# Hash matmuls moved beside the row sums, two pairs ahead, in a hash-bucket attention kernel

## The chip, the cores and the metric

The kernel runs on one core of a Trainium2 chip. The metric is the device time of one launch in microseconds, the median of several runs. Each time is that of the core from launch to end; the profile's span, a little shorter, runs from the first to the last instruction.

## The reference

Two blocks follow each other. The first is attention for 4 batches and 8 heads, 768 positions and 64 dimensions a head, in which a query sees only the keys of its own hash bucket:

```python
q_bits = (np.einsum('bhsd,dk->bhsk', q, proj) > 0)      # proj: 64 x 6
k_bits = (np.einsum('bhsd,dk->bhsk', k, proj) > 0)
q_bucket, k_bucket = (np.sum(b * 2 ** np.arange(6), axis=-1) for b in (q_bits, k_bits))
scores = np.where(q_bucket[..., :, None] == k_bucket[..., None, :], q @ k.T / 8, -1e9)
attn = softmax(scores);  attn_out = attn @ v
```

The second is a feed-forward block on the 3072 rows of 512 that come out of it:

```python
h = x @ w_in                                   # 512 -> 2048
g = h * (1.0 / (1.0 + np.exp(-1.702 * h)))
out = g @ w_out                                # 2048 -> 512
```

## The kernel before

Attention works on 16 **pairs** of heads: pair n holds two heads of one batch, head j on partitions 64j to 64j+63. The 768 queries of a pair are cut into two **halves** c of 384, its keys into 6 tiles of 128. The main loop (line 553) runs over pairs 1 to 15; pair 0 is written out ahead of it, interleaved with the start of pair 1's work. After the loop the feed-forward part takes over, which uses a seven-product scheme in two stages (lines 712 and 824) and keeps its own order.

The order of instructions on TensorE, VectorE, ScalarE and GpSimd is that of the program text, since the kernel turns the scheduler off for these four (`tc.manual_schedule(engines=ORDERED)`, line 72). SyncE's queue, which issues nearly all loads, is filled by the framework; its issues run in order too, so a load that waits holds up those behind it.

What one pair needs, by the names of the code:

- `fetch(n, name)` (line 317) loads the pair's keys or queries as rows, into one buffer for each of the two. `fetch_v(n)` (line 330) loads values, into two buffers in turn.
- `turn(n, name)` (line 388): VectorE transposes them in 32 x 32 blocks to columns, kT and qT, which have two buffers each (`wk`, bufs=2). The buffer of pair n+2 is that of pair n.
- `measure(n, name)` (line 393): ScalarE squares and sums the raw rows. It serves a guard at the end (`guard`, line 516), which picks another form of softmax if the inputs are very large.
- `hashed(n)` (line 402): four TensorE matmuls of 128 x 32, one for each quarter of the 128 columns (keys and queries, both halves), with the weights `pf`. They write the PSUM tile `hash`, of the pool `mps` that has one bank.
- `featured(n)` (line 411): VectorE makes 0 or a large number of each dot product (`f`), and eight small DMAs bring `f` to the layout of the score matmuls, kf and qf. These have two buffers, `feats[n % 2]`.
- `scores(n, c, tiles)` (line 423): for each key tile, two bf16 matmuls of the features (they add a large positive number where buckets agree) and two f32 matmuls of keys and queries, each on 64 rows of the array, into the PSUM tile `ps` (two banks; the pool `sps` has three such tiles). ScalarE then takes the exponential into `es[c]` (line 433).
- `add_low` and `add_high` (lines 437 and 443) add the exponentials over the key tiles: GpSimd the first three (lines 440, 441), VectorE the other three and GpSimd's sum (lines 446, 448), into `acc`.
- `values(n, c, tiles)` (line 450): 12 f32 matmuls of 128 x 64 into the PSUM tile `av`, for c = 0 in the one bank of the pool `aps`, for c = 1 in the bank of `mps`, which it shares with the hash. `unload(n, c)` (line 466) is ScalarE's copy of `av` into `xT`.
- `total(n)` (line 472): four matmuls of 128 x 32 with a matrix of ones, which sum `acc` over partitions into `dn`, in the bank of `aps`. Its first two need add_high of c = 0, the others that of c = 1.
- `invert(n)` (line 481) turns `dn`, takes reciprocals and turns them back into `rs`; `norm(n)` (line 497) multiplies `xT` by it, all on VectorE.
- `begin(n)` and `step(n, 6)` (lines 508, 504) convert one chunk of w_in per pair from 64-bit to 32-bit numbers: a load, then six VectorE instructions (lines 178 to 198) and one on ScalarE (line 190) that waits for the second of them.

TensorE in pair n of the loop runs scores of both halves, hash of pair n+1, values of both halves, sums. The few lines that set VectorE's order around them:

```python
inverted = invert(n - 1)
next(inverted)
if 1 < n < last:
    turn(n + 1, "k")
whole(inverted)
...
if n < last:
    turn(n + 1, "q")
add_high(n, 0)
if n < last:
    hashed(n + 1)
    featured(n + 1)
...
    norm(n - 1)
add_high(n, 1)
```

Of the kernel before, what the change touches and what calls it, by code (L numbers as in the profile page):

```python
# [19 lines left out]
P = 128  # L20
# [18 lines left out]
def kernel(  # L39
# [243 lines left out]
    def attention(ff):  # L283
# [4 lines left out]
        with actx:  # L288
# [28 lines left out]
            def fetch(n, name):  # L317

                b, hp = pairs[n]
                x = raws[n, name] = ld.tile([P, S // 32, 32], F32, tag=name, name=name)  # L320
                if (n, name) == (2, "q"):
                    behind(x[:, 0, 0:1])
                src = {"k": k, "q": q}[name]
                for j in range(2):
                    rows = src[b, 2 * hp + j].rearrange("(s p) (a i) -> a p s i", p=32, i=32)
                    for a in range(D // 32):
                        r0 = D * j + 32 * a
                        loader[0].dma_start(out=x[r0 : r0 + 32], in_=rows[a])
# [59 lines left out]
            def turn(n, name):  # L388
                x = raws[n, name]
                xt = xts[n, name] = wk.tile([P, S], F32, tag=f"{name}T", name=f"{name}T")  # L390
                nc.vector.transpose(xt, x.rearrange("p s i -> p (s i)"))

            def measure(n, name):

                x = raws.pop((n, name))
                i = 2 * n + "kq".index(name)
                junk = st.tile([P, S], BF16, tag="junk", name="junk", bufs=1)
                nc.scalar.activation(junk, x.rearrange("p s i -> p (s i)"), Act.Square, accum_out=sizes[:, i : i + 1])
# [3 lines left out]
            def hashed(n):  # L402

                h = dots[n] = mps.tile([P, HS], F32, tag="m", name="hash")
                for i, x in enumerate("kq"):
                    for c in range(2):
                        r0 = D * i + 32 * c
                        nc.tensor.matmul(h[r0 : r0 + 32, :], pf[x], xts[n, x][:, c * HS : (c + 1) * HS],  # L408
                                         start=True, stop=True)

            def featured(n):
                f = wk.tile([P, HS], BF16, tag="f", name="f", bufs=1)
                nc.vector.tensor_scalar(f, dots.pop(n), above[:, 0:1], weight[:, 0:1], op0=Alu.is_gt, op1=Alu.mult)
                for c in range(2):
                    for i, x in enumerate("kq"):

                        queue = nc.scalar if (n, x, c) == (1, "q", 0) else nc.sync
                        for j in range(2):
                            r0 = D * i + 32 * c + 2 * NB * j
                            queue.dma_start(out=feats[n % 2][x][D * j : D * j + 2 * NB, c * HS : (c + 1) * HS],  # L420
                                            in_=f[r0 : r0 + 2 * NB, :])

            def scores(n, c, kts):
                qT, kT, qf, kf = xts[n, "q"], xts[n, "k"], feats[n % 2]["q"], feats[n % 2]["k"]
                cols = slice(c * HS, (c + 1) * HS)
                for kt in kts:
                    ps = sps.tile([P, 2, 512], F32, tag="s", name="ps")
                    keys = slice(kt * P, (kt + 1) * P)
                    for a, m, last in ((kf, qf, False), (kT, qT, True)):
                        for j in range(2):  # L430
                            hs = slice(D * j, D * (j + 1))
                            nc.tensor.matmul(ps[:, j, 0:HS], a[hs, keys], m[hs, cols], start=not last, stop=last)  # L432
                    nc.scalar.activation(es[c][:, kt, :, 0:HS], ps[:, :, 0:HS], Act.Exp, scale=1.0 / D**0.5)  # L433
# [16 lines left out]
            def values(n, c, kts):  # L450
                if 0 in kts:

                    pool, tag = (mps, "m") if c else (aps, "av")
                    avs[n, c] = pool.tile([P, HS + 1], F32, tag=tag, name="av")
                av, vt = avs[n, c], vts[n]
                for t in kts:
                    for j in range(2):
                        nc.tensor.matmul(av[D * j : D * (j + 1), :], vt[:, t, j, :], es[c][:, t, j, :],  # L458
                                         start=(t == 0), stop=(t == T - 1))
# [6 lines left out]
            def unload(n, c):  # L466
                av = avs.pop((n, c))
                vs = st.tile([P, 1], F32, tag="vs", name="vs")
                nc.scalar.copy(vs, av[:, HS : HS + 1])
                nc.scalar.activation(x_of(n)[:, c * GT : (c + 1) * GT, :], av[:, 0:HS].rearrange("p (t s) -> p t s", t=GT), Act.Identity, bias=vs[:, 0:1])  # L470

            def total(n):

                dn = accs[n] = aps.tile([P, HS], F32, tag="av", name="dn")
                for c in range(2):
                    acc = accs.pop((n, c))
                    for j in range(2):
                        r0 = D * j + 32 * c
                        nc.tensor.matmul(dn[r0 : r0 + 32, :], ones[:, 0:32], acc[:, j, :], start=True, stop=True)  # L479

            def invert(n):


                rt = st.tile([P, HS // 32, 32], F32, tag="rt", name="rt", bufs=1)
                nc.vector.transpose(rt.rearrange("p s i -> p (s i)"), accs.pop(n))
                yield
                r = st.tile([P, 2, HS // 32], F32, tag="r", name="r")
                nc.vector.reciprocal(r, rt[:, :, 0].unsqueeze(1).to_broadcast([P, 2, HS // 32]))
                for r0 in range(0, P, 32):
                    c = r0 // 32 % 2  # L490
                    r1 = r0 + 32 - 64 * c
                    nc.vector.reciprocal(r[r1 : r1 + 32, c], rt[r0 : r0 + 32, :, 0])
                rs = accs[n] = st.tile([P, S], F32, tag="rs", name="rs", bufs=1)
                nc.vector.transpose(rs.rearrange("p (s i) -> p s i", i=32),
                                    r.rearrange("p c s -> p (c s)").unsqueeze(2).to_broadcast([P, S // 32, 32]))

            def norm(n):
                x, rs = x_of(n), accs.pop(n)
                nc.vector.tensor_tensor(x, x, rs.rearrange("p (t s) -> p t s", t=T), op=Alu.mult)  # L499
# [4 lines left out]
            def step(n, count=1):  # L504
                for _ in range(count):
                    next(conv.get(n, iter(())), None)
# [40 lines left out]
            fetch(2, "q")  # L547
            fetch_v(1)
            scores(0, 1, high)
            values(0, 1, low)  # L550
            values(0, 1, high)
            unload(0, 1)
            for n in range(1, last + 1):
                scores(n, 0, every)
                add_low(n, 0)
                if n == 1:
                    add_high(0, 1)
                    turn(2, "k")
                    total(0)
                inverted = invert(n - 1)  # L560
                next(inverted)
                if 1 < n < last:
                    turn(n + 1, "k")
                whole(inverted)
                if n == last:
                    guard(0)
                scores(n, 1, every)
                add_low(n, 1)
                if n < last:
                    turn(n + 1, "q")  # L570
                add_high(n, 0)
                if n < last:
                    hashed(n + 1)
                    featured(n + 1)
                    for x in "kq":
                        measure(n + 1, x)
                else:
                    guard(1)
                if n < last:
                    norm(n - 1)  # L580
                add_high(n, 1)
                if n == last:
                    norm(n - 1)
                values(n, 0, every)
                unload(n, 0)
                step(n, 6)
                values(n, 1, every)
                unload(n, 1)
                total(n)
                if n + 2 <= last:  # L590
                    for x in "kq":
                        fetch(n + 2, x)
                if n < last:
                    fetch_v(n + 1)
                    begin(n + 1)
                if n > last - len(x_sums):
                    x_sums[n - last - 1]()
# [378 lines left out]
    def whole(steps):  # L976
        for _ in steps:
            pass
# [46 lines left out]
```

## Time and profile before

| What | Value |
|---|---|
| Time, median of 3 runs | 875.63 us (875.22 to 876.58) |
| Span of the profiled run | 873.4 us |
| Attention, first instruction to the first feed-forward matmul | 321.2 us |
| TensorE busy | 862.0 us |
| VectorE busy | 718.4 us |
| ScalarE busy | 312.1 us |
| GpSimd busy | 321.4 us |
| Granted TensorE clock | 0.996 of full speed |

In the profile PE is TensorE's matmuls, PEld its weight loads, DVE VectorE, ACT ScalarE, POOL GpSimd and SP SyncE. A line of the matmul records gives the start and length in us, the engine, the line of the code, the operation, what it writes and reads, the rows and columns of the array that it uses (128*32 is a tile of all rows and 32 columns), the size and the count. An f32 matmul leaves two records. An entry in square brackets is idle time of the engine just before, and what ended it. The chain of work that ended last is followed back from the last instruction to whatever released each step; in order of time it shows which engine the end of the kernel hung on at each moment.

### The profile page before, as it was taken

The page shows a single profiled execution, that of the slowest core. Times are in us where ns is not written, and L with a number is a line of the kernel's source. Part 1 is how long each engine was busy: PE and PEld are TensorE (multiplying, and loading weights), DVE is VectorE, ACT ScalarE, POOL GpSimd, SP SyncE. Part 2 cuts the span into 40 slices and gives each one's busy share as a digit, 9 for nine tenths or more (in the row PEclk, how much of TensorE's full clock was granted, in tenths as well). Part 3 has the DMA queues.
Part 4 walks back from the last instruction along what each step waited for, and adds up shares of the span by engine and source line. Part 5 has one row for each costly group of instructions (what it writes and reads, how often), then busy time and mean ns, then how long its engine had stood idle before and what let it go on. Part 6 is the DMA issues. An engine that isn't in the chain of part 4 may idle for free.

```text
span 873.4 us, 11818 instructions
## 1 busy us (share of the span) xinstructions
PE 862.0 (99%) x4077; PEld 501.8 (57%) x4077; DVE 718.4 (82%) x1020; ACT 312.1 (36%) x519; POOL 321.4 (37%) x275
## 2 busy tenths in 40 slices
PE   9999999999999999999999999999999999999995
PEld 5444444444444444444444444444888888888884
DVE  4579999998999988778777778888888977897785
ACT  5756577777666653222233222332000000000000
POOL 4243334334433375665543344659903100000000
PEclk9999999999999999999999999999999999999998
DMA  5334456544444304565455555575844675467524
GB/s 133 59 59 84 84 102 101 117 89 83 83 84 91 75 25 158 192 217 193 175 193 185 205 181 202 183 249 184 298 167 155 197 250 197 163 200 241 193 97 99
DMA packets 169155, 131.99 MB, mean 151 GB/s; under 512 B 123616, under 2 KB 138112, under 8 KB 163712
## 3 DMA queue, kind: packets, MB, share of 16 engines
q1 hardware_dynamic: 166528, 129.70, 51.6%
q10 hardware_dynamic: 2560, 1.46, 0.7%
q8 instruction: 34, 0.56, 0.3%
q14 instruction: 33, 0.27, 0.1%
HBM read 79.69 MB, written 50.33 MB: 149 GB/s over the span
## 4 chain that ended last, share of the span: by engine, by line
PE 96%; DVE 3%; issue 0%; ACT 0%; ACTq 0%; DVEq 0%
PE product L712 33%; PE product L824 27%; PE ps L432 18%; PE av L458 14%; PE dn L479 1%; PE hash L408 1%; DVE xT L828 1%; PE tp L366 1%; DVE y L804 1%; DVE acc L448 0%; DVE xT L499 0%; PE warm L359 0%; PE hash L373 0%; DVE acc L446 0%; ACT e L433 0%
## 5 line engine op out<-in xcount | busy, mean ns | idle before, releaser
L433 ACT ACTIVATE e<-ps 128x768 f32<-128x768 f32 x192 | 150.6, 812 | 17.2 <-PE ps L432 14.9
L432 PE MATMUL ps<-qT,kT 64*128 64x384 f32 x768 | 155.1, 483 | 0.0
L712 PE MATMUL product<-xT,w_in_sb 128*128 128x512 f32 x288 | 135.5, 593 | 0.0
L458 PE MATMUL av<-e,v 128*64 128x385 f32 x768 | 128.2, 488 | 0.0
L440 POOL TENSOR_TENSOR acc<-e 128x768 f32<-128x768 f32 x32 | 51.3, 1604 | 192.2 <-ACT e L433 116.9
L720 ACT ACTIVATE c<-c 128x512 f32<-128x512 f32 x72 | 45.3, 630 | 184.9 <-issue 78.6
L458 PEld LDWEIGHTS av<-e,v 128*64 128x64 f32 x768 | 53.9, 136 | 72.8 <-issue 71.9
L712 PEld LDWEIGHTS product<-xT,w_in_sb 128*128 128x128 f32 x288 | 54.7, 190 | 68.9 <-issue 64.2
L712 PE MATMUL product<-t_x,s_in 128*128 128x512 f32 x192 | 90.2, 592 | 0.0
L432 PEld LDWEIGHTS ps<-qT,kT 64*128 64x128 f32 x768 | 68.1, 188 | 38.3 <-issue 37.9
L219 POOL TENSOR_TENSOR v<-c,u 128x512 f32<-128x512 f32 x24 | 34.1, 1422 | 121.1 <-ACT c L720 121.1
L837 ACT COPY u<-product 128x256 f32<-128x256 f32 x21 | 7.8, 372 | 172.1 <-PE product L824 138.9
L441 POOL TENSOR_TENSOR acc<-acc,e 128x768 f32<-128x768 f32 x32 | 64.1, 2002 | 2.5
L432 PE MATMUL ps<-qf,kf 64*128 64x384 bf16 x384 | 62.9, 324 | 0.1
L712 PEld LDWEIGHTS product<-t_x,s_in 128*128 128x128 f32 x192 | 36.5, 190 | 45.9 <-issue 43.7
L446 DVE SCALAR_TENSOR_TENSOR acc<-e 128x768 f32<-128x768 f32 x32 | 50.6, 1582 | 5.1 <-ACT e L433 5.1
L712 PE MATMUL product<-t_x,w_in_sb 128*128 128x512 f32 x96 | 45.1, 592 | 0.0
L712 PE MATMUL product<-xT,s_in 128*128 128x512 f32 x96 | 45.1, 592 | 0.0
L432 PEld LDWEIGHTS <-kf 64*128 64x128 bf16 x384 | 19.2, 94 | 35.1 <-issue 11.7
L448 DVE TENSOR_TENSOR acc<-acc,acc 128x768 f32<-128x768 f32 x32 | 31.2, 974 | 4.8 <-POOL acc L441 1.6
L824 PE MATMUL product<-raw_g,xT 128*128 128x256 f32 x152 | 35.1, 379 | 0.0
L448 DVE TENSOR_TENSOR acc<-acc,e 128x768 f32<-128x768 f32 x32 | 31.8, 995 | 3.8 <-ACT e L433 0.5
(207 smaller groups left out, 1495.1 us busy)
## 6 DMA issues: line engine op xcount, KB each, us to landing
raw_g<-g_dram SPq DMA_DIRECT2D x22, 1024.0 KB
s_in<-g_dram SPq DMA_DIRECT2D x20, 1024.0 KB
g_dram<-c SPq DMA_DIRECT2D x72, 256.0 KB
g_dram<-t SPq DMA_DIRECT2D x48, 256.0 KB
raw<-in_moe_w_in_dram SPq DMA_DIRECT2D x16, 512.0 KB
raw<-in_moe_w_out_dram SPq DMA_DIRECT2D x16, 512.0 KB
v<-in_v_dram SPq DMA_DIRECT2D x32, 192.0 KB
g_dram<-u SPq DMA_DIRECT2D x24, 256.0 KB
```

What stands on the lines that cost most here:

```text
L219: return [lambda: eng.tensor_tensor(t1, b12, b11, op=Alu.subtract), lambda: eng.tensor_tensor(b12, b22, b12, op=Alu.subtract), lambda: eng ...
L366: nc.tensor.matmul(tp[D * j : D * (j + 1), i * P : (i + 1) * P], x[name][:, j, c * GT + i, :], ident, start=True, stop=True)
L432: nc.tensor.matmul(ps[:, j, 0:HS], a[hs, keys], m[hs, cols], start=not last, stop=last)
L433: nc.scalar.activation(es[c][:, kt, :, 0:HS], ps[:, :, 0:HS], Act.Exp, scale=1.0 / D**0.5)
L440: nc.gpsimd.tensor_tensor(acc, es[c][:, 0, :, 0:HS], es[c][:, 1, :, 0:HS], op=Alu.add)
L441: nc.gpsimd.tensor_tensor(acc, acc, es[c][:, 2, :, 0:HS], op=Alu.add)
L446: nc.vector.scalar_tensor_tensor(acc, e[0], T * TINY, e[1], op0=Alu.add, op1=Alu.add)
L448: nc.vector.tensor_tensor(acc, acc, x, op=Alu.add)
L458: nc.tensor.matmul(av[D * j : D * (j + 1), :], vt[:, t, j, :], es[c][:, t, j, :], start=(t == 0), stop=(t == T - 1))
L712: nc.tensor.matmul(ps, wq[LEFT[i]][:, kc, :], xq[RIGHT[i]][:, kc, :], start=(kc == 0), stop=(kc == K2 - 1))
L720: nc.scalar.activation(c, c, Act.Gelu_apprx_sigmoid)
L824: nc.tensor.matmul(ps, wq[LEFT[i]][:, c, :], gq[RIGHT[i]][:, c, :], start=(c == 0), stop=(c == F4 - 1))
```

## The change

The hash of a pair is computed two pairs ahead instead of one, and its matmuls stand directly ahead of the matmuls of the sums, which use the array in the same tiles. So that the turned keys and queries are there two pairs ahead, both turns move to the phase of the second half ("on columns"), after add_high(n,0), and norm(n-1) moves from there into the phase of the first half ("on rows"), after the inversion. The raw keys and queries are then fetched three pairs ahead, and values are fetched ahead of the features on the queue. Since the hash's bank is in use for longer, av of the second half takes one of the three score tiles in pairs 1 to 13. Pair 1 does the work of catching up: hash(2) in the old place, hash(3) in the new one.

```diff
             def measure(n, name):
-                x = raws.pop((n, name))
+                x = raws[n, name]
...
             def values(n, c, kts):
                 if 0 in kts:
-                    pool, tag = (mps, "m") if c else (aps, "av")
-                    avs[n, c] = pool.tile([P, HS + 1], F32, tag=tag, name="av")
+                    if c and n == 0 or c and n + 2 > last:
+                        avs[n, c] = mps.tile([P, HS + 1], F32, tag="m", name="av")
+                    elif c:
+                        avs[n, c] = sps.tile([P, 2, 512], F32, tag="s", name="av1")[:, 0, 0 : HS + 1]
+                    else:
+                        avs[n, c] = aps.tile([P, HS + 1], F32, tag="av", name="av")
...
             scores(0, 1, high)
+            measure(2, "k")
...
                 if n == 1:
                     add_high(0, 1)
-                    turn(2, "k")
+                    for x in "kq":
+                        turn(2, x)
+                    fetch(3, "k")
                     total(0)
-                inverted = invert(n - 1)
-                next(inverted)
-                if 1 < n < last:
-                    turn(n + 1, "k")
-                whole(inverted)
+                    measure(2, "q")
+                    fetch(3, "q")
+                    fetch_v(2)
+                whole(invert(n - 1))
+                norm(n - 1)
                 if n == last:
                     guard(0)
                 scores(n, 1, every)
                 add_low(n, 1)
-                if n < last:
-                    turn(n + 1, "q")
                 add_high(n, 0)
-                if n < last:
-                    hashed(n + 1)
-                    featured(n + 1)
+                if n == 1:
+                    hashed(2)
+                    featured(2)
+                if n + 2 <= last:
                     for x in "kq":
-                        measure(n + 1, x)
-                else:
+                        turn(n + 2, x)
+                        measure(n + 2, x)
+                if n == last:
                     guard(1)
-                if n < last:
-                    norm(n - 1)
                 add_high(n, 1)
-                if n == last:
-                    norm(n - 1)
                 values(n, 0, every)
                 unload(n, 0)
                 step(n, 6)
+                if n + 3 <= last:
+                    for x in "kq":
+                        fetch(n + 3, x)
+                if 1 < n < last:
+                    fetch_v(n + 1)
                 values(n, 1, every)
                 unload(n, 1)
+                if n + 2 <= last:
+                    hashed(n + 2)
                 total(n)
                 if n + 2 <= last:
-                    for x in "kq":
-                        fetch(n + 2, x)
+                    featured(n + 2)
                 if n < last:
-                    fetch_v(n + 1)
                     begin(n + 1)
```

## The prediction

> **What bounds the kernel now.** I read the page first for busy shares and for the chain that ended last, then the chain in order of time, then the matmuls one by one where the chain leaves TensorE or changes what it does.
>
> ```profile
> PE 862.0 (99%) x4077; PEld 501.8 (57%) x4077; DVE 718.4 (82%) x1020; ACT 312.1 (36%) x519; POOL 321.4 (37%) x275
> ...
> PE 96%; DVE 3%; issue 0%; ACT 0%; ACTq 0%; DVEq 0%
> ```
>
> TensorE is busy for 99% of the span and is 96% of the chain; VectorE's 82% is an average over both halves. So the time can fall only where TensorE waits or spends time without streaming, and can rise only where it is made to wait. The chain in order of time, start, length, what:
>
> ```profile
> 50.01 0.97 DVE acc L448
> 50.98 0.04 issue
> 51.02 0.84 PE dn L479 x4
> 51.86 9.80 PE ps L432 x72
> 61.66 0.78 PE hash L408 x8
> 62.44 7.92 PE av L458 x48
> 70.35 0.78 PE dn L479 x8
> 71.13 9.80 PE ps L432 x72
> ```
>
> This is the steady state: from pair 2 on, every pair is 9.80 + 0.78 + 7.92 + 0.78 = 19.28 us of TensorE with nothing between, up to 321.16 us, where the feed-forward part starts. Nothing the diff edits runs later than the first microseconds of that part. The one place behind 12 us where attention leaves TensorE is the end of pair 1, at 39.7 to 51.0 us of the chain, which comes back to TensorE at 51.02.
>
> Inside a block there are small steps. The matmuls where scores end, hashes run and values begin (start, length, engine, line, op, tile, shape, count):
>
> ```profile
> 118.68 0.81 PE L432 MATMUL ps<-qT,kT 64*128 64x384 f32 x4
> 119.42 0.52 PE L408 MATMUL hash<-kT,pf_k 128*32 128x384 f32 x2
> 119.43 0.52 PE L408 MATMUL hash<-qT,pf_q 128*32 128x384 f32 x2
> 119.76 0.49 PE L408 MATMUL hash<-kT,pf_k 128*32 128x384 f32 x2
> 119.78 0.49 PE L408 MATMUL hash<-qT,pf_q 128*32 128x384 f32 x2
> 120.20 0.54 PE L458 MATMUL av<-e,v 128*64 128x385 f32 x2
> ```
>
> Look at starts, not lengths. The hash is two rounds on four column groups; round two starts 0.34 after round one. A third round would start at 120.10, but the values start at 120.20. So 0.10 of the block's 0.78 is the change from 128*32 tiles to 128*64. The same holds for the sums (dn starts at 128.12, the next scores at 128.90: 2 x 0.34 + 0.10), and the score block: 12 tiles at the 0.807 from start to start is 9.68, and 0.12 remains of 9.80. A pair has four such changes. Where scores hand over to values directly, in pair 0, it is no dearer: its blocks of three tiles take 2.53 = 3 x 0.807 + 0.11.
>
> **What the Trainium skill says.** "TensorEngine Tiling (Array Packing)", Key Properties: changing the tiling mode, not merely the tile, drains TensorE. The trace agrees: 0.10 to 0.12 us at each change, and 0.34 from round to round within a mode, where 384 columns are streamed. "Perfetto Trace Analysis", Tensor Engine Instruction: TensorE's end times are estimated. The trace agrees (a 0.52 matmul is followed after 0.34 in the same group), which is why I use starts. "SBUF — State Buffer", Who interferes with whom: VectorE and GpSimd share a port pair under an exclusive lock. The trace agrees: line 446 takes 0.92 us alone, and 2.43 when it starts at 122.36 beside GpSimd's add at 121.70.
>
> **The change part by part.**
>
> *Hash beside the sums.* Before, hash(n+1) lies between scores and values in pairs 1 to 14: scores, hash, values, sums, four mode changes. After, hash(n+2) comes just ahead of the sums: scores, values, hash, sums. Both are 128*32, so one change goes. Pair 1 still has hash(2) in the old place and gets hash(3) in the new one; pairs 2 to 13 have one in the new place; pair 14 has none. The number of hashes stays 14, and 13 of them have moved. A mode change that has no row of its own in this place is bounded: 0 saved if hash and sums still part by 0.10, 0.12 if the dearest change goes. I take 0.10, since round to round within a mode is plain in the trace: 13 x 0.10 = **1.3 us**.
>
> *The end of pair 1.* Here the sums wait:
>
> ```profile
> 49.87 0.84 PE L479 MATMUL dn<-acc,ones 128*32 128x384 f32 x4
> 51.02 0.84 PE L479 MATMUL dn<-acc,ones 128*32 128x384 f32 x4 [0.31 <-DVE acc L448]
> 51.79 0.34 PE L432 MATMUL ps<-qf,kf 64*128 64x384 bf16 x2
> ```
>
> The sums take 51.79 - 49.87 = 1.92 instead of 0.78: 1.14 lost, though only 0.31 is called idle, because the second half of the rows comes after the first and not beside it. It waits for VectorE's add_high(1,1), ready at 50.97. In the new order VectorE does turn(2,q) (0.94) in the 3.63 us in which it now waits for the first sums, then from 36.35: inversion to 39.2 (as now); norm(0), 1.4 with GpSimd idle (its 2.61 includes 1.2 behind GpSimd's add of 43.63 to 45.17), to 40.6; add_high(1,0), 3.0, to 43.6; features 0.7, to 44.3; the two turns of pair 3, 1.9, to 46.2; add_high(1,1), 3.0, plus 0.7 behind GpSimd's second add, to 49.9. TensorE now puts hash(3) first, so it reaches the sums at 49.87 + 0.68 = 50.55, and the result is there 0.6 earlier. I take the whole **1.14**; the bounds are 0 and 1.14. The keys for turn(3) are asked for when turn(2,k) is done (32.7), behind the values of pair 1, which end on the queue at 34.7, and the queries after measure(2,q) (37.4); in the trace a turn could start 2.6 us after the last issue of such a load, so by 42.5, ahead of 44.3.
>
> *Turns and norm swapped on VectorE.* The same instructions as before. A pair costs VectorE 17.5 to 18.2 us:
>
> ```profile
> core 0: us, PE busy (x) PEld busy (x) DVE busy (x) ACT busy (x) POOL busy (x), PEclk, DMA share, GB/s
> ...
> 109.69:128.97 19.28, 19.28 (x138) 9.01 (x140) 17.92 (x24) 13.62 (x23) 7.04 (x4) 1.00 0.55 95
> ```
>
> The new waits: turn(n+2) writes the buffers that scores(n,1) read, so it must wait for their end, 9.8 us into the pair. Behind it stand add_high(n,1), the conversion of w_in and f(n+2). VectorE comes to it at about 10.6: conversion to 2.6, f, inversion, norm and add_high(n,0), 0.7 + 2.8 + 1.4 + 3.1 later. From there 1.9 + 3.0 to 4.5 bring add_high(n,1) to 15.5 to 17, and the sums need it at 18.5. So no wait reaches TensorE: **0**. The waits that go (up to 0.9 for the hash, 0.2 to 0.7 for keys) were VectorE's own and buy nothing either.
>
> *av of the second half in a score buffer.* The third score tile of the next pair now waits until ScalarE has unloaded av, 1.6 us into the pair. Before, that unload ended at 110.69, 1.07 into the pair, held up by line 190, which waits for VectorE's conversion; the new order brings that conversion forward. **0**, with 0.5 us of room even if it does not.
>
> *Loads.* Values and the next keys go ahead of the features on the queue; features are needed a whole pair later than they are issued (16 us ahead, not 8). **0**. The first pair's measure(2,k) and measure(2,q), 1.03 each, move into ScalarE's waits (0.95 before the second half's first exponential, and before the unload at 30.8). **0**.
>
> Sum: 875.63 - 1.3 - 1.14 = **873.2 us**.
>
> **The rivals.**
>
> *Half of it.* If the sums of pair 1 still wait as long: 875.63 - 1.3 = 874.3. If hash and sums still drain between each other but the wait goes: 875.63 - 1.14 = 874.5. For the first: that moment depends on where GpSimd's locks fall, and two turns are added ahead of it. Against: 0.6 us of room. For the second: a wait on TensorE's own semaphore stands between hash and sums in the program; against: what it waits for is av of the first half, done 4 us before.
>
> *VectorE becomes the bound.* Its slack is 19.18 - 17.9 = 1.3 per pair. If the new order makes add_high(n,0) also meet GpSimd's add (0.92 to 2.43, plus 1.5) and leaves 0.4 of gaps, a pair takes 17.9 + 1.9 = 19.8, 0.6 too long for 12 pairs: 873.2 + 7.4 = 880.6, slower. For it: norm moves next to GpSimd's first adds. Against: those end about 6 us into the pair, when norm is just starting, and norm leaves the place where it was blocked.
>
> **Numbers.** Forecast 0.66, half of it 0.22, VectorE bound 0.12. The first gives 872.5 to 873.9, the second up to 874.8; with 0.2 either side, the range 872.3 to 875.0 leaves out the third and little else. 0.2% is 1.75 us, so the bar is 873.88: the forecast clears it by 0.7, both halves miss it. Faster 0.66, same 0.22, slower 0.12.
>
> **What would show it.** Right: pairs of 19.18 on the chain (9.80, 7.92, then 1.46 for hash and sums), sums starting 0.34 after the hash's second round, no TensorE idle about 50 us, the feed-forward part starting near 318.7. Wrong: hash and sums still 1.56 together; sums with an idle time ended by acc L448; scores waiting for the unload of av; VectorE with no idle in a pair and pairs above 19.28.

## The result, and the profile after

| | before | after |
|---|---|---|
| time, median (lowest to highest), us | 875.64 (874.88–876.58, 6 runs) | 871.63 (871.17–871.79, 6 runs) |
| ratio, 95% interval | | 0.9954 [0.9941, 0.9967] |
| span of the profiled execution, us | 873.43 | 869.93 |
| VectorE busy, us | 718.4 | 722.4 |

The kernel is 4.0 us faster; the forecast was 2.4. TensorE is still busy for 99% of the span and is still 96% of the chain that ended last. Cut at three instructions on TensorE and VectorE, the two profiled spans compare like this (head: to the first score matmul; attention: from there to the first feed-forward matmul; feed-forward: to the end of the last transpose into y; tail: to the end of the span):

| us | head | attention | feed-forward | tail |
|---|---|---|---|---|
| before | 10.53 | 310.57 | 544.96 | 7.38 |
| after | 10.81 | 307.64 | 545.00 | 6.48 |
| difference | +0.28 | **−2.93** | +0.04 | **−0.90** |

The 0.28 of the head is within its scatter: the profiles of before and of the six kernels built on it have heads of 9.74 to 11.24 (mean 10.53), and those of after and its five 9.97 to 10.81 (mean 10.42). What is left, 2.93 + 0.90 = 3.83, agrees with the gain of 4.0 within its interval (2.9 to 5.2).

**Attention** on the chain of waits of after, in order of time (start, us, engine, tile, line, count):

```profile
41.52 0.78 PE hash L408 x8
42.31 7.92 PE av L463 x48
50.22 0.78 PE hash L408 x8
51.01 0.65 PE dn L484 x8
51.65 9.80 PE ps L432 x72
61.45 7.92 PE av L463 x48
69.36 0.78 PE hash L408 x8
70.15 0.65 PE dn L484 x8
...
318.52 288.60 PE product L722 x672
```

Pair 1 has two hashes, at 41.52 and 50.22, and goes from its values straight into hash and sums, with no wait on VectorE. From then on a pair is 9.80 + 7.92 + 0.78 + 0.65 = 19.15 on the chain; from the first sums to the next on the timeline it is 19.14, against 19.28 before. Feed-forward starts at 318.52 instead of 321.16 (less the 0.28 of the head, 2.93 earlier). The block of hash and sums on TensorE's timeline (start, length, line, tile, shape, count):

```profile
107.57 0.52 PE L408 MATMUL hash<-kT,pf_k 128*32 128x384 f32 x2
107.59 0.52 PE L408 MATMUL hash<-qT,pf_q 128*32 128x384 f32 x2
107.92 0.49 PE L408 MATMUL hash<-kT,pf_k 128*32 128x384 f32 x2
107.93 0.49 PE L408 MATMUL hash<-qT,pf_q 128*32 128x384 f32 x2
108.24 0.83 PE L484 MATMUL dn<-acc,ones 128*32 128x384 f32 x8
109.00 0.34 PE L432 MATMUL ps<-qf,kf 64*128 64x384 bf16 x2
```

Read the starts: 107.57, 107.92, 108.24, and 109.00 for the next scores. The first round takes 0.35 to the second, but the second takes only 0.32 to the third. That third is the first round of the sums, another tile, another line, and no step between. Hash and sums together are 109.00 − 107.57 = 1.43; before they were 0.783 + 0.785 = 1.568.

**VectorE** waits in all of 51 to 300 us for these (what waits, for what; us in total, times, longest). First the two largest waits of before, then all of after:

```profile
DVE kT L391 <- DMA k<-in_k_dram: 7.3, 10, 3.2
DVE f L413 <- PE hash L408: 4.4, 8, 0.6
```

```profile
DVE f L413 <- DMA qf<-f: 1.9, 1, 1.9
DVE acc L448 <- POOL acc L441: 1.6, 1, 1.6
```

The two waits of before, 11.7 us over some 13 pairs, are gone. VectorE's advance over TensorE is seen in the room between the end of VectorE's last sum and the start of the dn matmuls that read it. In pairs 2 to 13 this room was 0.5 to 1.4 us before (0.54 and 0.60 in pairs 2 and 3) and is 2.15 in almost every pair now. In pair 1 it was −1.09 (TensorE waited) and is 0.26.

**The tail.** The two kernels end on the same operations. The last transpose into y, and the span with its mean clock, first of before and then of after:

```profile
865.42 0.63 DVE L804 STREAM_TRANSPOSE y<-xT 128x256 f32<-128x256 f32 x1
...
core 0: 873.4 us, clock 0.996
```

```profile
862.82 0.63 DVE L814 STREAM_TRANSPOSE y<-xT 128x256 f32<-128x256 f32 x1
...
core 0: 869.9 us, clock 0.997
```

From the end of this transpose to the end of the span it is 7.38 before and 6.48 after. The difference shows at the barrier that closes the program, where the engines wait for each other; it stands in the trace's semaphore records and in no line of the page. In before, SyncE, ScalarE and TensorE pass the barrier at 871.87 and VectorE only at 873.09, 1.22 later; in after all four pass it at 869.35 to 869.36. An instruction fetch lies close to the barrier in both (872.19 and 869.41), so its presence alone does not tell the two apart.

### The profile page after: what moved, and what is told of

It is laid out like the page before. It is cut to its first block, busy times and chain, and to the rows that moved or that the text cites. A ratio compares the mean times of both kernels' runs of the same rounds, so it can differ in the third digit from the quotient of the medians.

```text
span 869.9 us, 11937 instructions
## 1 busy us (share of the span) xinstructions
PE 859.7 (99%) x4077; PEld 502.2 (58%) x4077; DVE 722.4 (83%) x1020; ACT 313.4 (36%) x519; POOL 312.7 (36%) x275
## 3 DMA queue, kind: packets, MB, share of 16 engines
q10 hardware_dynamic: 2560, 1.46, 0.8%
## 4 chain that ended last, share of the span: by engine, by line
PE 96%; DVE 3%; issue 0%; ACTq 0%; ACT 0%; DVEq 0%
PE product L722 33%; PE product L834 26%; PE ps L432 18%; PE av L463 15%; PE hash L408 1%; PE dn L484 1%; DVE y L814 1%; DVE xT L838 1%; PE tp L366 1%; DVE t_x L838 0%; PE warm L359 0%; PE hash L373 0%; DVE t2a L221 0%; DVE raw_g L220 0%; DVE v L838 0%
## 5 line engine op out<-in xcount | busy, mean ns | idle before, releaser
L441 POOL TENSOR_TENSOR acc<-acc,e 128x768 f32<-128x768 f32 x32 | 55.7, 1740 | 2.5
L446 DVE SCALAR_TENSOR_TENSOR acc<-e 128x768 f32<-128x768 f32 x32 | 48.8, 1524 | 5.1 <-ACT e L433 5.1
L448 DVE TENSOR_TENSOR acc<-acc,e 128x768 f32<-128x768 f32 x32 | 34.4, 1075 | 3.3
```

The source lines that it names most:

```text
L441: nc.gpsimd.tensor_tensor(acc, acc, es[c][:, 2, :, 0:HS], op=Alu.add)
L446: nc.vector.scalar_tensor_tensor(acc, e[0], T * TINY, e[1], op0=Alu.add, op1=Alu.add)
L448: nc.vector.tensor_tensor(acc, acc, x, op=Alu.add)
```

## The experiments

The theory formed on these readings has three terms: 1.78 us (13 pairs x 0.137) from changes of the array's mode, that is, of the tile shape in which TensorE works; 1.14 from pair 1's wait, which stays away only because VectorE got room in the later pairs too; and 0.90 from where VectorE's instruction stream happens to end. Rivals: VectorE owes the 1.14 in any case and only the place is new; the tail is scatter or depends on the loads; the hash's distance of two pairs pays by itself. Each kernel is one edit of before or of after; ratios are to before, timed on the same chip.

**1 and 2. The tail.** Into a branch that is never taken, VectorE instructions are added: 68 in before, which is by how many the change makes VectorE's program longer, and 60 in after, which makes 128 together. Nothing that runs is changed.

```diff
     with tc.If(unsafe, preferred_fallthrough_block=False):
+        for _ in range(68):     # 60 in the kernel after
+            nc.vector.memset(ones[0:1, 0:1], 1.0)
         with tc.tile_pool(name="cv3", bufs=1) as cv:
```

> The kernel before, with 68 tiny VectorE memsets in the branch that is never taken: nothing that runs is changed, only where the end of VectorE's instruction stream lies (68 is by how many instructions the change makes it longer). Theory of the tail (VectorE waits about 1.2 us for its last instructions to be fetched): 1.2 us off, 874.4 us, and in the profile VectorE's last semaphore instruction comes as early as the other engines'. Rival (the rest of the gain is scatter in how loads land at the start and stores at the end): no change, 875.6 us.

> The changed kernel, with 60 such memsets in the branch that is never taken, which puts VectorE's end where it was before, modulo 128 instructions. Theory of the tail: 1.2 us back, 872.8 us. Rival (scatter): 871.6 us.

Measured: before with 68 is 874.49, ratio 0.9989 [0.9981, 0.9998], its tail 6.48 where it was 7.38 and its attention 310.58. After with 60 is 872.28, ratio 0.9964 [0.9951, 0.9978], its tail 7.35, its attention 307.64. The times alone show the first of the two; the interval of the second overlaps that of after. The tails show both, before with 68 first and after with 60 second:

```profile
865.37 0.63 DVE L804 STREAM_TRANSPOSE y<-xT 128x256 f32<-128x256 f32 x1
...
core 0: 872.5 us, clock 0.997
```

```profile
861.94 0.63 DVE L814 STREAM_TRANSPOSE y<-xT 128x256 f32<-128x256 f32 x1
...
core 0: 869.9 us, clock 0.997
```

So 0.9 us of this change is no effect of the new order: dead instructions give it to the old kernel and take it from the new one. All 13 profiles of this document sort the same way. Six have tails of 7.13 to 7.38 and VectorE 0.9 to 1.2 late at the barrier; seven have 6.36 to 6.52 and VectorE in time. The six are those in which the VectorE instructions on record and the dead ones add up to before's 1437, or to 128 more (after with 60, and experiment 6). That fits a period of 128, but only four sums occur (1437, 1464, 1505 and 1565). Through what the hardware arrives at this step stays open; what is shown is that the length of the stream decides it.

**3. Two more mode changes.** The kernel after, with the hash between the halves of the values.

```diff
-                values(n, 1, every)
-                unload(n, 1)
                 if n + 2 <= last:
                     hashed(n + 2)
+                values(n, 1, every)
+                unload(n, 1)
                 total(n)
```

> The changed kernel, with hash(n+2) between the two halves of the values instead of ahead of the sums: two changes of the array's tiles more in each of 13 pairs. If a change costs the 0.10 us of the prediction: pairs of 19.34, 13 x 0.20 = 2.6 slower, 874.2 us. If it costs 0.14 (with the slower first round after it): pairs of 19.42, 13 x 0.28 = 3.7 slower, 875.3 us. If the changes are not what counts: 871.6 us.

Measured: 875.69, ratio 1.0003 [0.9994, 1.0011]; attention 311.68. A steady pair on the chain:

```profile
100.59 4.03 PE av L463 x24
104.62 0.78 PE hash L408 x8
105.41 4.03 PE av L463 x24
109.44 0.78 PE dn L484 x8
110.22 9.79 PE ps L432 x72
```

By starts this is 9.794 + 4.034 + 0.783 + 4.034 + 0.785 = 19.43, against 19.14 in after: 0.29 for two changes more, 0.14 each. That is the same 0.14 from the other side, with the hash still two pairs ahead, so the distance as such pays nothing on TensorE. Attention is 4.04 longer than after: 13 x 0.288, and 0.29 that the hash waits in pair 1.

**4. Which of the two goes first.** The kernel after with total(n) ahead of hashed(n + 2), still neighbours.

```diff
-                if n + 2 <= last:
-                    hashed(n + 2)
                 total(n)
                 if n + 2 <= last:
+                    hashed(n + 2)
                     featured(n + 2)
```

> The changed kernel, with the sums first and the hash behind them. If it is the neighbourhood that saves the change of tiles, pairs 2 to 13 stay at 19.14 us, and only pair 1's sums, now 0.67 earlier, wait for add_high(1,1) again, about 0.5: 872.1 us. If the order of the two matters, 13 x 0.14 = 1.8 come back: 873.4 us.

Measured: 872.13, ratio 0.9965 [0.9953, 0.9977]. Pairs 2 to 13 are 19.14 as without the swap (sums 0.67, hash 0.76). Attention is 308.10, 0.46 longer, all in pair 1, where VectorE's result now comes 0.42 after the first sums start: the hash ahead of the sums is what covered it. Being neighbours gives the 0.14; the order gives pair 1 the last 0.46 of its 1.14.

**5. Pair 1's wait taken away without the rest.** Before, with norm(0) moved behind the addition that the sums of pair 1 wait for.

```diff
-                if n < last:
+                if 1 < n < last:
                     norm(n - 1)
                 add_high(n, 1)
-                if n == last:
+                if n in (1, last):
                     norm(n - 1)
```

> The kernel before, with norm(0) alone moved behind add_high(1,1), so that VectorE has the sums of pair 1 ready 2.6 us earlier. Theory: the 1.14 us that the sums of pair 1 lose go, 874.5 us, and pair 1's sums take 0.78 instead of 1.92. Rival (the wait moves to the features or to GpSimd's add): 875.6 us.

Measured: 875.67, ratio 1.0001 [0.9993, 1.0010]. In pair 1 the sums take 0.785, the wait is gone, and nothing is won: attention 310.70. VectorE's timeline shows where it went:

```profile
50.61 0.58 DVE L485 STREAM_TRANSPOSE rt<-dn 128x384 f32<-128x384 f32 x1
55.37 0.98 DVE L391 STREAM_TRANSPOSE kT<-k 128x768 f32<-128x768 f32 x1 [4.18 <-DMA k<-in_k_dram]
```

and TensorE's, at the end of pair 2:

```profile
68.95 1.28 PE L479 MATMUL dn<-acc,ones 128*32 128x384 f32 x8
70.16 0.34 PE L432 MATMUL ps<-qf,kf 64*128 64x384 bf16 x2
```

VectorE idles 4.18 us for the keys of pair 3, which are asked for at a fixed place in the text, and is then late for the sums of pairs 2 and 3: 1.21 and 1.14 instead of 0.785, and the scores after them 0.23 and 0.26 longer. Together that is 1.27, for the 1.14 saved. In before the room in these two pairs was 0.54 and 0.60, less than the 1.14 by which TensorE now came earlier.

**6. The same, with that load brought forward.** Before, as in 5, with the row measures of pair 2 done earlier and the keys and queries of pair 3 fetched earlier; the old places of both are left out in pair 1 (124 dead instructions keep the tail as it was).

```diff
             scores(0, 1, high)
+            measure(2, "k")
...
                     turn(2, "k")
+                    fetch(3, "k")
                     total(0)
+                    measure(2, "q")
...
                     turn(n + 1, "q")
+                if n == 1:
+                    fetch(3, "q")
```

> The kernel before, with norm(0) behind add_high(1,1) and also keys and queries of pair 3 fetched in pair 1 as soon as those of pair 2 are turned and measured (plus 124 memsets in the branch never taken, which keep the end of VectorE's stream where it was, modulo 128). Theory (the wait at the end of pair 1 needs both VectorE's time and the earlier loads to go for good): no wait in pairs 1 to 3, attention 1.14 shorter, 874.4 us. Rival (VectorE owes this time in any case and the wait shows up in a later pair): 875.5 us.

Measured: 875.45, ratio 0.9998 [0.9989, 1.0006]. Pairs 1 to 13 run without a wait. The bill comes in pair 14: sums 2.03, hash and scores 0.06 and 0.20 longer, 0.07 more in pair 15, attention 311.00.

```profile
PEld dn L479 <- DVE acc L448: 1.1, 1, 1.1
```

```profile
284.06 2.59 DVE L220 TENSOR_TENSOR xT<-xT 128x1024 f32<-128x1024 f32 x1
```

The first of these is the wait of the sums of pair 14, the second an addition of VectorE ahead of it. The same addition in before took 1.22 us. Next to it stands an addition of GpSimd, in this run and then in before:

```profile
284.03 1.54 POOL L440 TENSOR_TENSOR acc<-e 128x768 f32<-128x768 f32 x1 [7.12 <-ACT e L433]
```

```profile
285.62 1.22 DVE L220 TENSOR_TENSOR xT<-xT 128x1024 f32<-128x1024 f32 x1
...
285.85 2.39 POOL L440 TENSOR_TENSOR acc<-e 128x768 f32<-128x768 f32 x1 [7.39 <-ACT e L433]
```

Whichever started second took longer: VectorE 2.59 instead of 1.22, GpSimd 2.39 instead of 1.54. That agrees with the exclusive lock between the two engines of which the Trainium skill tells ("SBUF — State Buffer", Who interferes with whom). In this run GpSimd came 1.82 us earlier than in before and VectorE only 1.56, so VectorE started 0.03 behind GpSimd's addition instead of 0.23 ahead of it. In before the room at the sums of pair 14 was 0.47, so 1.37 more is a wait of TensorE. In the old order the time saved in pair 1 was thus lost again twice, in other places and for other reasons: late keys in experiment 5, a lost race with GpSimd here. What the two have in common is that the room there was smaller than 1.14. The rival, that VectorE owes the time in any case, foresaw both times but is not shown by them, and experiment 7 speaks against it.

**7. VectorE given room in the old order.** Before without norm(0) to norm(13): the outputs of pairs 0 to 13 stay unscaled, which frees some 2 us of VectorE in each pair and moves nothing else (14 dead instructions keep the tail).

```diff
-                if n < last:
-                    norm(n - 1)
                 add_high(n, 1)
```

> The kernel before, without norm(0) to norm(13): the attention outputs of pairs 0 to 13 are left unscaled, about 1.5 to 2.6 us of VectorE's work less per pair (and 14 memsets in the branch never taken, which keep the end of VectorE's stream in place). Theory (VectorE's lack of slack in the old order is why the wait at the end of pair 1 can't simply be moved): no wait in any pair, attention 310.57 - 1.14 = 309.43 us, 874.5 us. Rival (late keys hold up pairs 2 and 3 whatever VectorE does): waits remain there, about 875.5 us.

Measured: 874.22, ratio 0.9984 [0.9977, 0.9990]; attention 309.70. The 1.14 of pair 1 is gone, and only 0.27 comes back, in pair 3. Less work on VectorE makes the saving last, although VectorE waits longer for keys here than in before (7.3 us in the same stretch):

```profile
DVE kT L391 <- DMA k<-in_k_dram: 20.8, 13, 4.4
```

This run has the mode changes, load order and tail of before, and stands for most of the second term by itself. What it leaves open is which part of the change gives VectorE its room in after: the place of the turns, that of norm, or the earlier loads. No run separates them.

**8. The value tile in a score buffer alone.** Before, with the tile choice of after in values().

```diff
-                    pool, tag = (mps, "m") if c else (aps, "av")
-                    avs[n, c] = pool.tile([P, HS + 1], F32, tag=tag, name="av")
+                    if c and n == 0 or c and n + 2 > last:
+                        avs[n, c] = mps.tile([P, HS + 1], F32, tag="m", name="av")
+                    elif c:
+                        avs[n, c] = sps.tile([P, 2, 512], F32, tag="s", name="av1")[:, 0, 0 : HS + 1]
+                    else:
+                        avs[n, c] = aps.tile([P, HS + 1], F32, tag="av", name="av")
```

> The kernel before, with av of the second half in a score tile in pairs 1 to 13, and nothing else. Expected by the prediction: no change, 875.5 us, since the unload ends 0.5 us before the third score tile needs the room. Rival (scores wait for the unload): a wait in each of 13 pairs, with 0.3 us each 879 us.

Measured: 875.64, ratio 0.9998 [0.9990, 1.0007]; attention 310.58 against 310.57. It costs nothing and brings nothing; it makes the bank of the hash free for the new place.

**9. Hash beside the sums, one pair ahead only.** Before with 8, and hash and features of n + 1 moved down to just ahead of the sums of n. The neighbourhood is that of after, the distance that of before.

```diff
                 if n < last:
-                    hashed(n + 1)
-                    featured(n + 1)
...
                 unload(n, 1)
+                if n < last:
+                    hashed(n + 1)
+                    featured(n + 1)
                 total(n)
```

> The kernel before, with hash(n+1) directly ahead of the sums but still only one pair ahead (av of the second half in a score tile). The change of tiles is saved, but the next pair's scores need the features: after the hash come 0.7 us on VectorE and two of four rounds of small DMAs (3.0 us to issue, about 2 to land), at least 5 us of wait in 14 pairs, 945 us; if VectorE's conversion runs first, 8 us in 14 pairs, 985 us. If the features were off the path: 873 us.

Measured, one run: 973.08; attention 408.56, nearly 98 more. The waits from 100 to 140 us, two pairs:

```profile
PEld L432 <- DMA kf<-f: 10.1, 4, 3.9
PE ps L432 <- DMA qf<-f: 9.6, 4, 4.8
```

Scores wait for the features, which go from VectorE through eight small transfers on the queue. On TensorE's starts the scores come 3.9 to 5.3 us late in each of the 14 pairs, 61 us in all. Then they take 2.1 to 3.6 too long, 39 us in all. The start of one block of scores, and the time about it (window, PE busy, PEld, DVE, ACT and POOL busy with counts, then clock, DMA share, GB/s):

```profile
109.54 0.34 PE L432 MATMUL ps<-qf,kf 64*128 64x384 bf16 x1 [4.09 <-DMA qf<-f]
110.27 0.47 PE L432 MATMUL ps<-qf,kf 64*128 64x384 bf16 x1 [0.38 <-DMA qf<-f]
```

```profile
105.00:109.50 4.50, 0.46 (x8) 0.09 (x1) 4.39 (x10) 0.00 (x0) 0.00 (x0) 1.00 0.03 6
110.00:112.00 2.00, 1.73 (x7) 1.15 (x8) 0.00 (x0) 0.00 (x0) 0.00 (x0) 0.50 0.04 9
```

A second wait inside the block, for the rest of the features, is 0.15 to 0.48 us, some 4 us in all. The other 35 us come from the clock. The 14 idle times ahead of the scores are 3.2 to 5.2 us long, and about the end of each the trace's clock record goes to 0.50 for 3.4 or 6.8 us. In the block shown that is from 109.71 to 113.13; half of these 3.4 us is 1.7, and the block is 2.1 too long with 0.38 of second wait. So nearly two thirds of the loss are waits, and the rest is what the waits do to the clock; the change of tiles that goes gives some 2 us back. This is what the distance of two pairs is for. It buys no time; it is the price of the place beside the sums, paid in advance.

**10. The values' load left behind the features.** The kernel after with fetch_v(n + 1) behind featured(n + 2).

```diff
-                if 1 < n < last:
-                    fetch_v(n + 1)
                 values(n, 1, every)
...
                     featured(n + 2)
+                if 1 < n < last:
+                    fetch_v(n + 1)
```

> The changed kernel, with fetch_v(n+1) behind featured(n+2) in the text. On the queue this puts the values of pair 3 and half of those of pair 4 behind the features; from pair 5 on the queue's order is as in the changed kernel. If loads on the queue wait behind features that wait for VectorE, the values of pairs 3 and 4 come 2 to 4 us late, and TensorE waits: 4 to 8 us slower, 876 to 880 us. If the place on the queue doesn't matter: 871.6 us.

Measured: 873.52, ratio 0.9974 [0.9963, 0.9985]; attention 309.80, 2.16 longer than after.

```profile
81.38 8.49 PE L463 MATMUL av<-e,v 128*64 128x385 f32 x48 [1.59 <-DMA v<-in_v_dram]
```

Only pair 3 is hit: its values start 1.66 late and run 0.51 longer, most of it a second wait. On the queue the two loads for pair 3 were issued at 78.26 and 78.82, behind the features at 71.92 to 76.73; in after they went at 67.88 and 68.40. Of pair 4, one load is behind the features too, at 97.76 for a use at 101.02, and nothing waits; from pair 5 on the loads go a pair ahead, as in after. Less than expected, and not nothing: the load's place is part of the change, worth 2 us.

**11. One more neighbourhood.** The kernel after, with the sums of pair 0, which still part the two halves of pair 1's scores, put beside the hash of pair 2; two changes, 0.28 us, would go.

```diff
                     fetch(3, "k")
-                    total(0)
...
-                whole(invert(n - 1))
-                norm(n - 1)
+                if n > 1:
+                    whole(invert(n - 1))
+                    norm(n - 1)
...
                 if n == 1:
+                    total(0)
                     hashed(2)
+                    inverted = invert(0)
+                    next(inverted)
                     featured(2)
+                    whole(inverted)
...
                 add_high(n, 1)
+                if n == 1:
+                    norm(0)
```

> The changed kernel, with the sums of pair 0 moved from between the two halves of pair 1's scores to the place directly ahead of hash(2), and VectorE's inversion and norm of pair 0 moved behind add_high(1,0). Two changes of the array's tiles less: 2 x 0.14 = 0.28 off attention (307.64 to 307.36), 871.4 us, as long as the values of pair 1 don't wait for the inversion to free the bank; if they do, the 0.28 is lost again or more.

Measured: 876.51, ratio 1.0011 [1.0004, 1.0017], 4.9 slower than after; attention 312.21. The expected 871.4 was wrong. The values of pair 1 on TensorE, and the granted clock while they ran (window, PE busy, PEld, DVE, ACT and POOL busy with counts, then clock, DMA share, GB/s):

```profile
45.22 9.45 PE L463 MATMUL av<-e,v 128*64 128x385 f32 x48 [3.09 <-DVE rt L490]
```

```profile
44.80:46.20 1.40, 0.98 (x4) 0.53 (x6) 1.35 (x5) 0.00 (x0) 1.39 (x1) 0.50 0.02 6
46.20:48.20 2.00, 2.00 (x8) 0.70 (x6) 1.94 (x5) 0.00 (x0) 1.82 (x2) 0.50 0.04 9
48.20:50.80 2.60, 2.60 (x18) 1.12 (x16) 2.50 (x4) 0.00 (x0) 0.00 (x0) 1.00 0.04 11
```

dn and the values of the first half share one buffer (tag "av"). dn must be read out by VectorE before the values can start, and VectorE came to it at 44.59, behind an addition. TensorE idled 3.09. The clock was then 0.50 up to 48.21, and the values took 9.38 instead of 7.92: the idle time cost 1.46 more. In experiment 10 an idle time of 1.59 left the clock at 1.00. The two mode changes did go, for 0.24, but the scores of pair 1 took 0.19 longer, for a reason that was not followed up. The expectation had named this wait as the case in which the gain is lost "or more", but its number took the other case, and it had no term for the clock.

No run beat the kernel after.

## Why the prediction was wrong in size and right in kind

It foresaw a gain through the two terms that it named, and both are there. The time falls below the stated range because one term was too small and one was missing, and the missing one weighs more. With the first put right the forecast would have been 875.63 − 1.78 − 1.14 = 872.7, still in the range; with 0.90 for the tail it comes to 871.8, and 871.63 was measured.

- **"I take 0.10 … 13 x 0.10 = 1.3"**: the term that was mis-sized. It measured 0.137 a pair, 1.78 in all. The step that failed is "round two starts 0.34 after round one", taken for the pace within a mode. It is the pace of the first round after a change (0.35 in after, from 107.57 to 107.92). Within a mode the pace is 0.322. So a hash by itself has 0.783 − 2 x 0.322 = 0.14 of change in it: a step of 0.11 behind it, and a first round 0.02 slower. The profile of before could have told: a pair's values are 24 rounds of 385 columns, and 7.92 / 24 is 0.33 with the change in it, so 384 columns within a mode can hardly take 0.34. The upper bound, "0.12 if the dearest change goes", was too low for the same reason: it counted the step and not the slower first round. Experiment 3 gives 0.14 from the other side. "TensorEngine Tiling (Array Packing)", Key Properties, in the Trainium skill says that TensorE drains at a mode change; the runs agree, and say how much.
- **"Nothing the diff edits runs later than the first microseconds of that part"**: the step that put the end of the kernel at nothing. It holds for the instructions that run, and feed-forward did not change (+0.04). But the change also makes VectorE's program 68 instructions longer, and with that the tail went from 7.38 to 6.48. Experiments 1 and 2 turn these 0.9 us on and off. That they came as a gain is luck: with 60 more dead instructions the same change has the long tail.
- **"I take the whole 1.14"**: right. The sums of pair 1 take 0.76 instead of 1.92. The working behind it had 0.6 us of room for VectorE there; it was 0.26, so it was a nearer thing than it looked, and without the hash in front it would have lost 0.46 (experiment 4).
- **"The waits that go … were VectorE's own and buy nothing either"**: wrong, though no microsecond of the sum hung on it by name. Experiments 5 and 6 show that the wait of pair 1, taken away there, comes back in pairs 2 and 3 or in pair 14 where VectorE's room is smaller than 1.14, and experiment 7 that it stays away for the most part when VectorE has less to do. The waits that went are 0.9 us a pair, and the room grew by 1.0 on the average of pairs 2 to 13; that the one is the source of the other is likely, and not tested by itself. The 1.14 was counted as the gain of one reordered spot, but it needed VectorE to be earlier in all the later pairs.
- **av in a score buffer, 0**: right (experiment 8). **Loads and features, 0**: right for the kernel as it stands, and not because they are free: 98 us hang on the distance of the features, a third of it through the clock, and 2.2 on the place of the values' load (experiments 9 and 10).
- **The rival "VectorE becomes the bound"**: wrong. It is busy for 18.16 of 19.14 us a pair, yet has 2.15 of room at the sums. Some 1.5 of the 18.16 is no work: an addition in each pair (line 446, at 158.96) takes 2.43 instead of 0.94, since it starts just behind one of GpSimd (158.89). **The rival "half of it"**: wrong in both forms; hash and sums don't drain between each other, 108.24 − 107.92 = 0.32.
- The signs that it named were these: sums 0.34 after the hash's second round (0.32), no idle at 50 us (none), feed-forward near 318.7 (318.52), pairs of 19.18 (19.14).

## What to carry to other kernels

Measure the pace within a mode between rounds two and three, not one and two, and count mode changes of TensorE by that: two small blocks of the same mode belong side by side. When a saved wait doesn't show in the time, look for it in the next places where the same engine can be late; it lasts only where that engine comes earlier by as much, or has more room than that. And before a few tenths of a per cent are credited to an idea, cut the span at fixed instructions, head, phases and tail: here a quarter of the gain lay where nothing was edited.

## What the runs showed of the hardware that I had not expected

- The end of a kernel depends on how many instructions VectorE has in its program, run or not: 68 dead ones took 0.90 us off the tail, and 60 put 0.87 back.
- A block of 128*32 rounds by itself costs 0.14 us more than next to another of the same kind: 0.11 is the step behind it, 0.02 lies in the slower first round.
- After an idle time of 3.1 us TensorE ran its first 3.0 us at a granted clock of 0.50 and lost another 1.46 (experiment 11). Each of the 14 idle times of 3.2 to 5.2 us in experiment 9 brought 3.4 or 6.8 us at 0.50, an estimated 35 us of loss on top of the waits. One of 1.59 brought none (experiment 10).
- An addition on VectorE took 1.22 us when it started 0.23 ahead of one on GpSimd, which then took 2.39; it took 2.59 when it started 0.03 behind, and GpSimd's 1.54. A shift of 0.26 us between the engines decided which of them lost a microsecond.
